# Block-sparse attention followed by a gated MLP: a written-out start for the first two head pairs, small copies moved to Pool, and six output buffers

## The chip, the cores and the metric

The kernel runs on one core of one Trainium2 chip. The metric is the time of one launch in device microseconds (us). Executions of one kernel mostly agree within 0.3%. "Faster" and "slower" mean by more than 2%.

The engines are called PE (TensorE, matmul), DVE (VectorE), ACT (ScalarE), Pool (GpSimd) and SP (SyncE, which here only issues DMAs).

## The reference

```
attention, B=4, H=8, S=768, D=64, chunks of 32 keys:
  k_min, k_max = min, max of k over each chunk
  ub = sum_d max(q*k_min, q*k_max)          # upper bound of a chunk's scores
  ub = -1e9 where the chunk lies after the query's own chunk
  the 6 chunks with the largest ub are kept
  attn = softmax(q k^T / 8 over kept, causal positions);  x = attn v
gated MLP on x (4, 768, 512):
  h = relu(x w_in);  u, v = halves of h
  v = layer-normalised v;  v = w_spatial v + b_spatial   (over the sequence)
  out = (u * v) w_out
```

## The kernel before

The 32 heads are handled as 16 pairs, four to a batch. Each pair has a **preparation** and a **main part**. A table of "beats" (12 to a pair) gives the program order; a scheduler then places the instructions on the engines, and for the first beats it keeps PE's order as written.

Preparation of a pair: PE transposes k; DVE takes the chunk maxima and minima of it (`kmm`); these are copied into a block-diagonal operand (`km`); PE transposes q; its positive and negative parts are taken (`rq`); PE multiplies them to the bounds (`ub`); DVE finds the top six and writes the selection next to q; PE transposes q with its selection, and a copy brings that to SBUF (`a`, two halves). The keys go into `kh`, whose other half holds a constant that turns the selection into a score penalty.

Main part: PE makes scores, ACT takes 12 exps (10 of 128x512 and 2 of 128x128), PE multiplies with v. The causal triangle inside the diagonal blocks is a matmul on PE in batch 0 (pairs 0 to 3), and a selection on Pool from pair 4 on.

```
def init_kh(i):                                   # the constant half of kh
    for hi, (d0, d1) in enumerate(HALF):
        if i < 2:
            nc.scalar.copy(kh_ring[i][hi][d0:d1, :], expand)
        else:
            nc.sync.dma_start(out=kh_ring[i][hi][d0:d1, :], in_=expand)

def k_bounds(self):                               # kmm -> km
    for hi, (d0, d1) in enumerate(HALF):
        copy = nc.gpsimd.tensor_copy if 2 <= self.i < 4 else nc.scalar.copy
        s0, s1 = HALF[1 - hi]
        copy(self.km[d0:d1, :, hi], self.kmm[s0:s1])

def a_copy(self, hi):
    if self.i >= 8: return                        # later pairs: DMA transpose
    copy = nc.vector.tensor_copy if self.i == 0 and hi == 0 else nc.scalar.copy
    copy(self.a[:, :, hi, :], self.tr.rearrange("d (t s) -> d t s", s=P))

def triangle(self, hi):
    if self.b == 0: return                        # batch 0: matmul on PE
    ...
    nc.gpsimd.affine_select(out=blk, in_=blk, ...)

def load_k(g, hi, xy=None):                       # all q, k, v, weight loads: Pool
    ...
    nc.gpsimd.dma_start(out=..., in_=source(k, b, h, 2))

def load_b():
    nc.sync.dma_start(out=b_col, in_=...)         # 768 values of four bytes

def o_group(ti):
    ...
    o_sb = ml.tile([P, DM], F32, tag="o", name="o", bufs=3)
    nc.scalar.copy(o_sb, o_ps)
    nc.sync.dma_start(out=out[b, ti * P:(ti + 1) * P, :], in_=o_sb)
```

The loads convert from 32 to 16 bits. That is why they all stand on Pool: the Trainium skill, "DMA: Bandwidth & Descriptors", section "SWDGE vs HWDGE vs iDMA", says that a DMA that casts can only be issued from GpSimd. The page of this kernel agrees in that its software queue carries all of these loads, 76,512 packets.

The softmax here doesn't subtract the row's maximum and nothing guards it: scores larger than these inputs give would overflow.

Of the kernel before, what the change touches and what calls it, by code (L numbers as in the profile page):

```python
# [10 lines left out]
F32 = mybir.dt.float32  # L11
# [5 lines left out]
P = 128  # L17
# [31 lines left out]
def kernel(  # L49
# [11 lines left out]
    nc = tc.nc  # L61
    B, H, S, D = q.shape
    NCH = S // CHUNK
    DM = H * D
# [14 lines left out]
    ml = ctx.enter_context(tc.tile_pool(name="ml", bufs=2))  # L79
# [14 lines left out]
    beats = defaultdict(list)  # L94

    def at(beat, fn, *args):
        beats[beat].append((fn, args))
# [4 lines left out]
    NB = 4  # L102
# [3 lines left out]
    kh_ring = [[ring.tile([P, S], F16, name=f"kh{i}_{hi}") for hi in range(2)] for i in range(NB)]  # L106
# [40 lines left out]

    def init_kh(i):
        for hi, (d0, d1) in enumerate(HALF):
            if i < 2:  # L150
                nc.scalar.copy(kh_ring[i][hi][d0:d1, :], expand)
            else:
                nc.sync.dma_start(out=kh_ring[i][hi][d0:d1, :], in_=expand)


    W = 2 * NCH
# [3 lines left out]
    class Pair:  # L160
# [26 lines left out]

        def k_bounds(self):
            for hi, (d0, d1) in enumerate(HALF):
                copy = nc.gpsimd.tensor_copy if 2 <= self.i < 4 else nc.scalar.copy  # L190
                s0, s1 = HALF[1 - hi]
                copy(self.km[d0:d1, :, hi], self.kmm[s0:s1])

        def k_operand(self, hi):
            d0, d1 = HALF[1 - hi]
            copy = nc.scalar.copy if self.i == 0 else nc.vector.tensor_copy
            copy(self.kh[hi][d0:d1], self.kT[d0:d1])

        def trans_tile(self):
# [10 lines left out]
        def q_parts(self, m):  # L210
            if m == 0:
                self.rq = sb.tile([P, 2, S], F16, tag="rq", name="rq")
                nc.vector.tensor_scalar(self.rq[:, 0, P:S], in0=self.tr[:, P:S], scalar1=0.0, scalar2=None, op0=Alu.max)
            elif self.i == 0:
                nc.scalar.activation(self.rq[:, 1, P:S], self.tr[:, P:S], func=Act.Relu, scale=-1.0)
            else:
                nc.vector.tensor_scalar(self.rq[:, 1, P:S], in0=self.tr[:, P:S], scalar1=-1.0, scalar2=0.0,
                                        op0=Alu.mult, op1=Alu.max)
# [37 lines left out]
        def a_copy(self, hi):  # L256
            if self.i >= 8:
                return
            copy = nc.vector.tensor_copy if self.i == 0 and hi == 0 else nc.scalar.copy
            copy(self.a[:, :, hi, :], self.tr.rearrange("d (t s) -> d t s", s=P))  # L260


# [109 lines left out]
        nc.vector.tensor_copy(wsT[:, so, :], tr)  # L372

    def load_b():
        nc.sync.dma_start(out=b_col, in_=moe_b_spatial.rearrange("(to ti) -> ti to", ti=P))

    def mlp(b):

        st = {}
        steps = []  # L380

        def matmuls(group, cols, operands, after=None, chunk=2):

            n = len(operands)
            for c0 in range(0, n, chunk):
                def go(c0=c0):
                    if c0 == 0:
                        st[group] = ml_tile()
                    for j in range(c0, min(c0 + chunk, n)):
                        lhsT, rhs = operands[j]()  # L390
                        mm(st[group][:, 0:cols], lhsT=lhsT, rhs=rhs, start=(j == 0), stop=(j == n - 1))  # L391
                    if c0 + chunk >= n:
                        after(st.pop(group))
                steps.append((cols * min(chunk, n - c0), go))

        def v_group(ti):
            def after(h):
                if ti == 0:
                    st["vraw"] = ml.tile([P, NQT, DH], F32, tag="vraw", name="vraw", bufs=1)
                    st["mv"] = ml.tile([P, NQT, nc.vector.BN_AGGR_DIM], F32, tag="mv", name="mv")  # L400
                nc.scalar.activation(st["vraw"][:, ti, :], h, func=Act.Relu)  # L401
                stats = ml.tile([P, nc.vector.BN_STATS_DIM], F32, tag="stats", name="stats")
                nc.vector.bn_stats(stats, st["vraw"][:, ti, :])  # L403
                nc.vector.bn_aggr(st["mv"][:, ti, :], stats)
            matmuls(("v", ti), DH, [lambda ko=ko: (xT[b][:, ko, ti * P:(ti + 1) * P], w_in_sb[:, ko, DH:DFF])
                                    for ko in range(NDO)], after)

        def norm_group(ti):
            def go():
                if ti == 0:  # L410
                    st["rstd"] = ml.tile([P, NQT, 1], F32, tag="rstd", name="rstd")
                    nc.scalar.activation(st["rstd"], st["mv"][:, :, 1:2], func=Act.Ln, bias=eps_t)
                    nc.scalar.activation(st["rstd"], st["rstd"], func=Act.Exp, scale=-0.5)  # L413
                    st["vn"] = ml.tile([P, NQT, DH], F16, tag="vn", name="vn", bufs=1)
                nc.vector.tensor_scalar(st["vn"][:, ti, :], in0=st["vraw"][:, ti, :], scalar1=st["mv"][:, ti, 0:1],  # L415
                                        scalar2=st["rstd"][:, ti, :], op0=Alu.subtract, op1=Alu.mult)
            steps.append((0, go))

        def u_group(ti):
            def after(h):  # L420
                if ti == 0:
                    st["u"] = ml.tile([P, NQT, DH], F16, tag="u", name="u", bufs=1)
                nc.scalar.activation(st["u"][:, ti, :], h, func=Act.Relu)  # L423
            matmuls(("u", ti), DH, [lambda ko=ko: (xT[b][:, ko, ti * P:(ti + 1) * P], w_in_sb[:, ko, 0:DH])
                                    for ko in range(NDO)], after)

        def s_group(ti):
            def after(vs):
                g = ml.tile([P, DH], F16, tag="g", name="g", bufs=3)
                nc.vector.scalar_tensor_tensor(g, in0=vs, scalar=b_col[:, ti:ti + 1], in1=st["u"][:, ti, :],  # L430
                                               op0=Alu.add, op1=Alu.mult)
                gT = st["gT", ti] = ml.tile([P, KO, P], F16, tag="gT", name="gT", bufs=NQT)
                nc.sync.dma_start_transpose(out=gT, in_=g)
            matmuls(("s", ti), DH, [lambda si=si: (wsT[:, si, ti * P:(ti + 1) * P], st["vn"][:, si, :])
                                    for si in range(NQT)], after)

        def o_group(ti):
            def after(o_ps):
                o_sb = ml.tile([P, DM], F32, tag="o", name="o", bufs=3)
                nc.scalar.copy(o_sb, o_ps)  # L440
                nc.sync.dma_start(out=out[b, ti * P:(ti + 1) * P, :], in_=o_sb)
            matmuls(("o", ti), DM, [lambda db=db: (st["gT", ti][:, db, :], w_out_sb[:, db, :])
                                    for db in range(KO)], after)

        def take(fn, *args):
            fn(*args)
            out, steps[:] = list(steps), []
            return out

        v_, u_, n_, s_, o_ = ([take(fn, ti) for ti in range(NQT)]  # L450
                              for fn in (v_group, u_group, norm_group, s_group, o_group))
        return v_, u_, n_, s_, o_


    B0 = -30
# [6 lines left out]
    at(B0, init_ring, 0)  # L462
    at(B0, init_small)
    at(B0, init_expand)
    at(B0, init_masks)
    at(B0, load_k, 0, 0, 1)
    at(B0, load_k, 0, 1, 1)
    at(B0, load_q, 0, 0, 1)
    at(B0, load_q, 0, 1, 1)
    at(B0, load_v, 0)  # L470
    at(B0, init_ring, 1)
    at(-6, init_ring, 2)
    for i in range(NB):
        at(B0 if i < 2 else -8, init_kh, i)
    at(40, load_b)
    for g in range(1, NPAIR // 2):
        t0 = 2 * g * BEATS
# [14 lines left out]
        at(t0 + 18, p.x_transpose)  # L492
    for i, p in enumerate(pairs):
        t0 = i * BEATS
        if i == 1:
            t0 += 4
        if i == 0:
            for step in ((p.k_transpose,), (p.k_max,), (p.k_min,), (p.k_operand, 0), (p.q_transpose,),
                         (p.q_parts, 0), (p.k_bounds,), (p.q_parts, 1), (p.k_operand, 1), (p.bounds,), (p.top, 0), (p.top, 1), (p.select,),
                         (p.a_transpose, 0), (p.a_copy, 0), (p.a_transpose, 1), (p.a_copy, 1)):  # L500
                at(B0 + 1, *step)
            continue
        at(t0 - 27, p.k_transpose)
        at(t0 - 22, p.k_max)
        at(t0 - 21, p.q_transpose)
        at(t0 - 20, p.k_min)
# [10 lines left out]
        at(t0 - 9, p.a_copy, 0)  # L517
        at(t0 - 7, p.a_transpose, 1)
        at(t0 - 6, p.a_copy, 1)
    for j in range(NDO):  # L520
        at(20 + 8 * j, load_w_in, j)
    for j in range(NQT):
# [30 lines left out]
            done += cost  # L553

    with tc.manual_schedule(engines={mybir.EngineType.PE}):
        for beat in sorted(b for b in beats if b < 0):
            for fn, args in beats.pop(beat):
                fn(*args)
    for beat in sorted(beats):
# [31 lines left out]
```

## Time and profile before

Median 211.34 us of three runs before the prediction (211.15 to 211.51); 211.43 with the runs made beside the changed kernel.

The page of the kernel before; busy us, share of the span, number of instructions of each engine:

```profile
PE 187.0 (89%) x1922; PEld 114.8 (55%) x1922; DVE 154.1 (74%) x453; ACT 155.7 (74%) x323; POOL 79.6 (38%) x99
```

An average hides the stages. The table of stretches of the kernel before: each row is a stretch in us, its length, then busy us (and instructions) of PE, PE weight loads, DVE, ACT, Pool, then the clock, DMA share and GB/s.

```profile
0.00:5.00 5.00, 0.00 (x0) 0.00 (x0) 3.34 (x12) 2.11 (x2) 3.79 (x9) 1.00 0.66 37
20.00:25.00 5.00, 3.95 (x59) 3.00 (x59) 4.96 (x21) 3.87 (x9) 2.30 (x4) 1.00 3.52 142
30.00:40.00 10.00, 8.47 (x152) 7.00 (x151) 8.45 (x31) 9.17 (x20) 7.09 (x11) 1.00 2.15 167
40.00:50.00 10.00, 8.84 (x129) 6.45 (x127) 8.86 (x32) 9.36 (x21) 7.66 (x9) 1.00 1.77 176
50.00:58.00 8.00, 7.29 (x103) 5.23 (x102) 6.59 (x15) 7.81 (x18) 7.25 (x9) 1.00 2.01 173
80.00:100.00 20.00, 20.00 (x225) 12.42 (x224) 18.62 (x53) 15.47 (x33) 7.62 (x8) 1.00 1.80 130
120.00:160.00 40.00, 40.00 (x403) 23.54 (x400) 31.41 (x91) 33.61 (x75) 6.63 (x8) 1.00 0.65 119
```

Three regimes: a start in which nothing is full; from about 17 to 58 us attention alone, with ACT and DVE the fullest (38.11 and 36.20 us busy of the 41.30 between 16.7 and 58); then, once the MLP joins in, PE without a gap. From 80 us on only less PE idle time, or less work, can help.

The timeline of the kernel before: start us, duration us, engine, line, operation, output<-input, and in brackets the idle time before and what ended it. First PE's q transposes of pair 0, then ACT from pair 0's last preparation step to pair 1's first exp, then Pool, then the tail.

```profile
9.60 0.69 PE L208 MATMUL trm<-identity,qs_83 128*128 128x128 f16 x5 [2.91 <-DMA qs_83<-in_q_dram]
...
14.99 0.80 ACT L260 COPY a<-trm 128x768 f16<-128x768 f16 x1 [2.76 <-PE trm L254]
16.70 1.57 ACT L274 ACTIVATE e<-sc 128x512 f16<-128x512 f32 x3 [0.90 <-PE sc L272]
18.30 0.48 ACT L192 COPY km_87<-kmm 64x48 f16<-64x48 f16 x2
18.80 2.78 ACT L274 ACTIVATE e<-sc 128x512 f16<-128x512 f32 x6
...
25.46 2.18 ACT L274 ACTIVATE e<-sc 128x512 f16<-128x512 f32 x4
...
50.73 2.04 POOL L330 DMA_DIRECT2D k<-in_k_dram  x2 [0.69 <-PE sc L269]
52.83 0.86 POOL L281 TENSOR_SCALAR_AFFINE_SELECT e<-e 128x768 f16<-128x768 f16 x1
...
202.25 0.59 ACT L440 COPY o<-mlp 128x512 f32<-128x512 f32 x1 [0.28 <-PE mlp L391]
204.32 1.79 ACT L440 COPY o<-mlp 128x512 f32<-128x512 f32 x3 [1.48 <-DMA out_dram<-o]
```

PE waits for q until 9.60; the first exp is at 16.70; the last three output copies wait 1.48 us for one of three buffers to be written out.

### The profile page before, as it was taken

The numbers are of one execution on the slowest core, as the hardware profiler recorded it, in microseconds if no ns is written. First come the engines' busy times: TensorE is split into PE (matmuls) and PEld (weight loads), VectorE is DVE, ScalarE is ACT, GpSimd is POOL, SyncE is SP. The second block draws the span as 40 slices with busy tenths as digits, with TensorE's granted clock in tenths as the row PEclk, the third lists the DMA queues.
The fourth block names the chain that finished last, engine by engine and source line by source line (L and its number), as shares of the span: only waits on it lengthen the run. The fifth ranks groups of instructions, "written<-read, shape, count | busy, mean of one in ns | idle before, by whom it ended". The sixth has DMA issues, their size and how long they took to land.

```text
span 209.2 us, 5074 instructions
## 1 busy us (share of the span) xinstructions
PE 187.0 (89%) x1922; PEld 114.8 (55%) x1922; DVE 154.1 (74%) x453; ACT 155.7 (74%) x323; POOL 79.6 (38%) x99
## 2 busy tenths in 40 slices
PE   0359799798999999999999999999999999999991
PEld 0256577575666665656664656556555554444440
DVE  6348989888889989899888799888547356366520
ACT  4638798999997899785979996668999821666033
POOL 7995697595991364237114111111111110000000
PEclk9999999999999999999999999999999999999998
DMA  6999999999999699979998932948792115530365
GB/s 38 158 128 155 141 172 155 181 177 173 172 163 165 50 117 125 152 128 123 155 258 183 175 55 50 128 86 148 192 172 66 38 28 100 179 147 3 75 157 219
DMA packets 115496, 27.66 MB, mean 132 GB/s; under 512 B 110352, under 2 KB 111888, under 8 KB 115472
## 3 DMA queue, kind: packets, MB, share of 16 engines
q0 software_dynamic: 76512, 12.19, 88.2%
q1 hardware_dynamic: 38960, 15.15, 36.0%
q8 instruction: 15, 0.25, 0.5%
q14 instruction: 9, 0.07, 0.1%
HBM read 24.38 MB, written 6.29 MB: 147 GB/s over the span
## 4 chain that ended last, share of the span: by engine, by line
PE 65%; ACT 17%; DVE 5%; POOL 5%; DMA 4%; issue 3%; POOLq 0%; ACTq 0%
PE mlp L391 38%; PE sc L269 11%; ACT e L274 9%; PE acc L292 8%; ACT a L260 3%; DMA k<-in_k_dram 3%; PE ub L225 2%; POOL qs_83 L341 2%; PE kTp L173 2%; PE tr L208 1%; DVE vn L415 1%; POOL k L332 1%; ACT o L440 1%; DMA out_dram<-o 1%; ACT u L423 1%
## 5 line engine op out<-in xcount | busy, mean ns | idle before, releaser
L274 ACT ACTIVATE e<-sc 128x512 f16<-128x512 f32 x192 | 97.2, 552 | 15.6 <-PE sc L269 13.7
L391 PE MATMUL mlp<-w_in_sb,xT 128*128 128x512 f16 x192 | 52.9, 379 | 0.0
L281 POOL TENSOR_SCALAR_AFFINE_SELECT e<-e 128x768 f16<-128x768 f16 x24 | 20.8, 867 | 68.7 <-ACT e L274 68.6
L292 PEld LDWEIGHTS <-e 128*128 128x128 f16 x672 | 31.6, 97 | 17.5 <-DVE x_2178 L300 1.0
L391 PE MATMUL mlp<-vn,wsT 128*128 128x512 f16 x144 | 37.3, 379 | 0.0
L440 ACT COPY o<-mlp 128x512 f32<-128x512 f32 x24 | 14.1, 590 | 20.8 <-PE mlp L391 18.6
L403 DVE BATCH_NORM_STATS2 stats<-vraw 128x6 f32<-128x512 f32 x24 | 16.6, 693 | 13.5 <-ACT vraw L401 13.1
L391 PE MATMUL mlp<-w_out_sb,gT 128*128 128x512 f16 x96 | 25.1, 379 | 0.0
L391 PEld LDWEIGHTS <-xT 128*128 128x128 f16 x192 | 17.2, 97 | 12.4 <-issue 0.4
L430 DVE SCALAR_TENSOR_TENSOR g<-mlp,b_col,u 128x512 f16<-128x512 f32 x24 | 17.9, 747 | 7.3 <-PE mlp L391 6.2
L391 PEld LDWEIGHTS <-wsT 128*128 128x128 f16 x144 | 12.9, 98 | 10.4
L181 DVE TENSOR_REDUCE kmm<-kTp 128x24 f16<-128x768 f16 x16 | 15.1, 945 | 3.4 <-PE kTp L173 3.2
L401 ACT ACTIVATE vraw<-mlp 128x512 f32<-128x512 f32 x24 | 14.4, 601 | 3.0 <-PE mlp L391 3.0
L423 ACT ACTIVATE u<-mlp 128x512 f16<-128x512 f32 x24 | 14.3, 597 | 1.7 <-PE mlp L391 1.5
L330 POOL DMA_DIRECT2D k<-in_k_dram x14 | 14.4, 1042 | 2.5 <-PE kTp L173 1.8
L185 DVE TENSOR_REDUCE kmm<-kTp 128x24 f16<-128x768 f16 x16 | 15.1, 943 | 0.0
L173 PE MATMUL kTp<-identity,k 128*128 128x128 f16 x96 | 8.6, 230 | 6.3 <-POOL tri L144 5.9
L391 PEld LDWEIGHTS <-gT 128*128 128x128 f16 x96 | 9.1, 98 | 8.9
L292 PE MATMUL acc<-vt_80,e 128*128 128x65 f16 x252 | 13.7, 193 | 0.0
L415 DVE TENSOR_SCALAR vn<-vraw,mv,rstd 128x512 f16<-128x512 f32 x24 | 11.8, 544 | 2.2 <-ACT rstd L413 2.1
L292 PE MATMUL acc<-vt_81,e 128*128 128x65 f16 x252 | 13.0, 193 | 0.2 <-DVE x_3135 L300 0.2
L299 DVE RECIPROCAL rec<-acc 128x6 f32<-128x6 f32 x32 | 6.0, 187 | 6.5 <-PE acc L292 6.2
(165 smaller groups left out, 337.5 us busy)
## 6 DMA issues: line engine op xcount, KB each, us to landing
out_dram<-o SPq DMA_DIRECT2D x24, 256.0 KB, 2.3
k<-in_k_dram POOLq DMA_DIRECT2D x14, 192.0 KB, 8.2
vt_80<-in_v_dram POOLq DMA_DIRECT2D x3, 384.0 KB, 8.7
qs_84<-in_q_dram POOLq DMA_DIRECT2D x6, 192.0 KB, 7.5
vt_81<-in_v_dram POOLq DMA_DIRECT2D x3, 384.0 KB, 8.8
ws_raw<-in_moe_w_spatial_dram POOLq DMA_DIRECT2D x6, 192.0 KB, 7.6
w_in_sb<-in_moe_w_in_dram POOLq DMA_DIRECT2D x8, 128.0 KB, 6.6
qs_85<-in_q_dram POOLq DMA_DIRECT2D x4, 192.0 KB, 7.2
```

The lines of the kernel that those rows point to most:

```text
L181: nc.vector.tensor_reduce(self.kmm[:, 0, :], self.kT.rearrange("d (c ch) -> d c ch", ch=CHUNK), axis=AX.X, op=Alu.max)
L185: nc.vector.tensor_reduce(self.kmm[:, 1, :], self.kT.rearrange("d (c ch) -> d c ch", ch=CHUNK), axis=AX.X, op=Alu.min, negate=True)
L269: mm(sc[:, col:col + n], lhsT=self.kh[hi][:, t * P:(t + 1) * P], rhs=self.a[:, q0 // P:(q0 + n) // P, hi, :], start=True, stop=not diag)
L274: nc.scalar.activation(out=self.e[hi][:, g * 512:g * 512 + width], in_=sc[:, 0:width], func=Act.Exp, scale=scale)
L281: nc.gpsimd.affine_select(out=blk, in_=blk, compare_op=Alu.is_ge, fill=0.0, base=0, channel_multiplier=-1, pattern=[[0, NQT], [1, P]])
L292: mm(self.av[:, qi, :], lhsT=self.e[hi][:, c:c + P], rhs=self.v[hi][:, t, 0:D + 1], start=first and n == 0, stop=last and n == len(blocks) ...
L330: nc.gpsimd.dma_start(out=t[:, :, :, 1 - hi, :].rearrange("p x t d -> p (x t) d"), in_=source(k, b, h, 2))
L391: mm(st[group][:, 0:cols], lhsT=lhsT, rhs=rhs, start=(j == 0), stop=(j == n - 1))
L403: nc.vector.bn_stats(stats, st["vraw"][:, ti, :])
L423: nc.scalar.activation(st["u"][:, ti, :], h, func=Act.Relu)
L430: nc.vector.scalar_tensor_tensor(g, in0=vs, scalar=b_col[:, ti:ti + 1], in1=st["u"][:, ti, :], op0=Alu.add, op1=Alu.mult)
L440: nc.scalar.copy(o_sb, o_ps)
```

## The change

The intent is to shorten the start and to take small work off ACT in the stretch where ACT is full. The core of the diff (the reordering of the beat table is cut):

```
 def init_kh(i):
-            if i < 2:
-                nc.scalar.copy(kh_ring[i][hi][d0:d1, :], expand)
-            else:
-                nc.sync.dma_start(out=kh_ring[i][hi][d0:d1, :], in_=expand)
+            nc.scalar.copy(kh_ring[i][hi][d0:d1, :], expand)
 def k_bounds(self):
-                copy = nc.gpsimd.tensor_copy if 2 <= self.i < 4 else nc.scalar.copy
+                copy = nc.gpsimd.tensor_copy if 1 <= self.i < 8 else nc.scalar.copy
 def a_copy(self, hi):
-            copy = nc.vector.tensor_copy if self.i == 0 and hi == 0 else nc.scalar.copy
+            copy = nc.vector.tensor_copy if self.i < 2 and hi == 0 else nc.scalar.copy
 def load_b():
-        nc.sync.dma_start(out=b_col, ...)
+        nc.gpsimd.dma_start(out=b_col, ...)        # now late, on Pool's queue
 def o_group(ti):
-                o_sb = ml.tile([P, DM], F32, tag="o", name="o", bufs=3)
+                o_sb = ml.tile([P, DM], F32, tag="o", name="o", bufs=6)
 beat table:
-    at(B0, init_masks) before pair 1's k loads;   + after them
-    pair 0 written out, pair 1 by the general table
+    pairs 0 and 1 written out as one list: pair 0's bounds and selection, init_kh(2), init_kh(3),
+    then pair 1's k work between pair 0's two q transposes, pair 1's q work from beat 0 on
-    PE order as written for beats below 0;        + for beats below 6
     [cut: pairs 2 and 3 prepared at other beats]
```

More of the change, by code (lines that the diff above doesn't have):

```diff
@@ L195, in k_operand @@
             d0, d1 = HALF[1 - hi]
-            copy = nc.scalar.copy if self.i == 0 else nc.vector.tensor_copy
+            copy = nc.scalar.copy if self.i < 1 else nc.vector.tensor_copy
             copy(self.kh[hi][d0:d1], self.kT[d0:d1])
@@ L213, in q_parts @@
                 nc.vector.tensor_scalar(self.rq[:, 0, P:S], in0=self.tr[:, P:S], scalar1=0.0, scalar2=None, op0=Alu.max)
-            elif self.i == 0:
+            elif self.i < 1:
                 nc.scalar.activation(self.rq[:, 1, P:S], self.tr[:, P:S], func=Act.Relu, scale=-1.0)
@@ L374, in load_b @@
     def load_b():
-        nc.sync.dma_start(out=b_col, in_=moe_b_spatial.rearrange("(to ti) -> ti to", ti=P))
+        nc.gpsimd.dma_start(out=b_col, in_=moe_b_spatial.rearrange("(to ti) -> ti to", ti=P))
     def mlp(b):
@@ L464 @@
     at(B0, init_expand)
-    at(B0, init_masks)
     at(B0, load_k, 0, 0, 1)
     at(B0, load_k, 0, 1, 1)
+    at(B0, init_masks)
     at(B0, load_q, 0, 0, 1)
@@ L471 @@
     at(B0, init_ring, 1)
-    at(-6, init_ring, 2)
-    for i in range(NB):
-        at(B0 if i < 2 else -8, init_kh, i)
+    at(B0, init_ring, 2)
+    at(B0, init_kh, 0)
+    at(B0, init_kh, 1)
     at(40, load_b)
@@ L494 @@
         t0 = i * BEATS
-        if i == 1:
-            t0 += 4
-        if i == 0:
-            for step in ((p.k_transpose,), (p.k_max,), (p.k_min,), (p.k_operand, 0), (p.q_transpose,),
-                         (p.q_parts, 0), (p.k_bounds,), (p.q_parts, 1), (p.k_operand, 1), (p.bounds,), (p.top, 0), (p.top, 1), (p.select,),
-                         (p.a_transpose, 0), (p.a_copy, 0), (p.a_transpose, 1), (p.a_copy, 1)):
-                at(B0 + 1, *step)
+        if i < 2:
             continue
-        at(t0 - 27, p.k_transpose)
+        t0 += 4 if i < 4 else 0
+        at(t0 - (22 if i < 4 else 27), p.k_transpose)
         at(t0 - 22, p.k_max)
@@ L519 @@
         at(t0 - 6, p.a_copy, 1)
+    p, n = pairs[0:2]
+    for beat, *step in (
+            (B0 + 1, p.k_transpose), (B0 + 1, p.k_max), (B0 + 1, p.k_min), (B0 + 1, p.k_operand, 0),
+            (B0 + 1, p.q_transpose), (B0 + 1, p.q_parts, 0), (B0 + 1, p.k_bounds),
+            (B0 + 1, p.q_parts, 1), (B0 + 1, p.k_operand, 1), (B0 + 1, p.bounds), (B0 + 1, p.top, 0),
+            (B0 + 1, p.top, 1), (B0 + 1, p.select), (B0 + 1, init_kh, 2), (B0 + 1, init_kh, 3), (B0 + 1, p.a_transpose, 0), (B0 + 1, p.a_copy, 0),
+            (B0 + 1, n.k_transpose), (B0 + 1, p.a_transpose, 1), (B0 + 1, n.k_max), (B0 + 1, p.a_copy, 1), (B0 + 1, n.k_min),
+            (B0 + 1, n.k_operand, 0),
+            (0, n.q_transpose), (1, n.q_parts, 0), (1, n.k_bounds), (1, n.q_parts, 1),
+            (1, n.k_operand, 1), (2, n.bounds), (3, n.top, 0), (3, n.top, 1), (4, n.select), (5, n.a_transpose, 0),
+            (5, n.a_copy, 0), (6, n.a_transpose, 1), (6, n.a_copy, 1)):
+        at(beat, *step)
     for j in range(NDO):
@@ L555 @@
     with tc.manual_schedule(engines={mybir.EngineType.PE}):
-        for beat in sorted(b for b in beats if b < 0):
+        for beat in sorted(b for b in beats if b < 6):
             for fn, args in beats.pop(beat):
```

## The prediction

> **What bounds the kernel now.** Busy table: PE 187.0 of 209.2 us; the 22 us of idle PE lie mostly at the front. Table of stretches and timeline show three regimes. (a) 0 to 16.7 us, start-up: the first exp starts at 16.70; PE waits 2.9 us for pair 0's q, until 9.6. (b) 16.7 to 58 us, attention alone: ACT about 94% busy, DVE nearly as full (4.96 and 4.97 of 5 us in 20:25 and 25:30; the chain of waits is DVE from 19.7 to 24). (c) 58 to 201 us: PE-bound (20.00 of 20, 40.00 of 40). At the end ACT waits 1.48 us for an output DMA (three buffers).
>
> Time taken out of (a) and (b) should carry to the end; nothing taken off ACT in (c) should.
>
> **The change, costed from the trace.**
> 1. Four SP copies of the key constants (96 KB each, issued 4.2 to 6.6 us) become four ACT copies of 0.83 us. They stand after pair 0's key operand (ends 12.2), where ACT idles 2.76 us before 14.99: nearly free. The bias load leaves the start too. The Trainium skill, "Trainium Kernel Development and Optimization", Key Constraints, says that DMAs of all queues share 16 engines and interleave; the trace fits: a q load of pair 0 beside those copies took 4.9 us, later ones 3.6 to 3.8. q may land up to 1 us earlier; I count 0.4.
> 2. PE order: the first scores come straight after pair 0's transposes instead of after pair 1's q transposes: gain 0.3. Against it, pair 1's bounds matmuls stand before the fourth score tile; ACT should wait about 1.3 us near 18 to 19.4.
> 3. Pair 1's first a-copy goes from ACT (0.80) to DVE (0.56), and pairs 1, 4, 5, 6, 7 send their bounds copies (2 x 0.24 us) to Pool. ACT loses 3.2 us in (b). As DVE is as full, I expect about half to count: pair 1's first exp from 25.46 to about 24.2, start of the MLP from 58.4 to about 56.
> 4. Pool waits in order for the key reductions, so some loads issue 1 to 2 us later; later pairs' loads have many us of slack.
> 5. Six output buffers take away the 1.48 us wait; PE then sets the last copies, which end about 205.45 instead of 206.11: gain 0.65.
>
> Sum: 0.7 (start) + 0.6 (pair 0 to pair 1) + 1.3 (rest of b) + 0.65 (tail) = 3.3 us.
>
> **Predicted time: 208.0 us, 8 in 10 between 205.8 and 210.3. Faster by over 2% (below 207.1) 0.29, within 2% 0.68, slower by over 2% 0.03.**
>
> **What would show it.** (1) The wait of the first q transposes ends before 9.3; first exp at 15.6 to 16.5. (2) An ACT gap of about 1.3 us after pair 0's third exp; pair 1's first exp near 24.2. (3) First ReLU of the MLP at about 56; ACT's bounds copies 18 instead of 28; DVE at least 95% busy between 15 and 40. (4) No PE wait over 1 us for a k, q or v load after 20 us. (5) No output copy waiting for an output DMA at the end; PE busy still about 187.
>
> **What would make it wrong.** Pool's in-order waits hold up a load that is needed. ACT's gap in pair 0 is larger, because pair 1's select or pair 2's k comes late. DVE alone sets the pace in (b), and the ACT savings buy nothing. Or q lands a full microsecond earlier and DVE keeps up: then about 206.

## The result, and the profile after

The changed kernel takes 209.04 us (median of four, 208.90 to 209.11) against 211.43 before. The ratio is 0.9884, with a 95% interval of 0.9865 to 0.9903. (A ratio here is the mean time of one kernel's fast runs over that of the other's of the same rounds, so not quite the ratio of the medians.) A later control, the same kernel on the chip of the last experiments, gave 0.9887. So it gained 2.4 us, inside the predicted range, less than the 3.3 us of the predicted sum.

The page of the changed kernel:

```profile
PE 189.0 (91%) x1922; PEld 115.4 (56%) x1922; DVE 154.5 (75%) x454; ACT 155.7 (75%) x316; POOL 82.6 (40%) x110
```

PE's busy time rose by 2.0 us with the same 1922 matmuls, while the kernel got faster. The Trainium skill, "Trainium Kernel Development and Optimization", section "Performance Expectations", warns that matmul busy time is a bad metric for how close a kernel is to roofline, because matmuls are pipelined. The busy time did not follow the work. PE busy is used below to see where PE is full, not as an amount of work.

The table of stretches of the changed kernel:

```profile
20.00:25.00 5.00, 4.61 (x69) 3.45 (x68) 4.82 (x13) 4.75 (x11) 3.84 (x8) 1.00 3.67 141
30.00:40.00 10.00, 9.08 (x137) 6.66 (x135) 9.89 (x36) 8.52 (x18) 8.03 (x14) 1.00 2.13 168
50.00:58.00 8.00, 6.94 (x101) 4.92 (x100) 6.36 (x21) 6.50 (x13) 6.61 (x10) 1.00 2.02 173
80.00:100.00 20.00, 20.00 (x220) 12.48 (x218) 18.73 (x53) 15.34 (x33) 6.86 (x7) 1.00 1.58 132
```

Two rows matter. In 30:40 DVE is now full (9.89 of 10) and ACT is not. In 50:58 ACT fell from 7.81 to 6.50, and no engine is full: something makes them wait.

The timeline of the changed kernel (its source lines are three lower than before's):

```profile
8.02 0.69 PE L205 MATMUL trm<-identity,qs 128*128 128x128 f16 x5 [1.48 <-DMA qs<-in_q_dram]
...
14.59 0.80 ACT L257 COPY a<-trm 128x768 f16<-128x768 f16 x1
15.29 0.60 ACT L271 ACTIVATE e<-sc 128x512 f16<-128x512 f32 x1
18.55 3.21 ACT L271 ACTIVATE e<-sc 128x512 f16<-128x512 f32 x7 [1.23 <-PE sc L266]
22.02 0.80 ACT L257 COPY a<-trm 128x768 f16<-128x768 f16 x1 [0.25 <-PE trm L251]
22.71 5.44 ACT L271 ACTIVATE e<-sc 128x512 f16<-128x512 f32 x12
...
50.85 2.04 POOL L327 DMA_DIRECT2D k<-in_k_dram  x2 [0.80 <-DMA k<-in_k_dram]
52.95 0.86 POOL L278 TENSOR_SCALAR_AFFINE_SELECT e<-e 128x768 f16<-128x768 f16 x1
53.86 0.36 PE L289 MATMUL acc<-vt,e 128*128 128x65 f16 x6 [0.55 <-POOL e L278]
54.48 1.09 ACT L271 ACTIVATE e<-sc 128x512 f16<-128x512 f32 x2 [1.34 <-PE sc L266]
...
202.60 0.58 ACT L437 COPY o<-mlp 128x512 f32<-128x512 f32 x1 [0.28 <-DMA out_dram<-o]
203.46 0.58 ACT L437 COPY o<-mlp 128x512 f32<-128x512 f32 x1 [0.28 <-PE mlp L388]
```

q is there at 8.02, the first exp starts at 15.29. (The 12 exps from 22.71 are the last two of pair 0 and the first ten of pair 1.) In the tail the copies are paced by PE: the 0.28 us gaps are those of the earlier copies, so the label of the first one does not name what set its start.

The lines at 50 to 55 us are the new thing. Read them from the bottom. ACT waits 1.34 us for pair 5's scores. Those stand behind six value matmuls of pair 4 in PE's queue, which wait for Pool's selection of the causal triangle. The selection stands in Pool's queue behind two key loads of 2.04 us in all. Those keys are for pairs 10 and 11; PE first reads them at 85.61 us. The chain of waits of the changed kernel (from the last instruction back, at each step to what released it) says the same. It adds that Pool stood idle for 0.80 us before those loads; this profile puts the wait down to the landing of an earlier key load (the control, 0.62 us, to PE's scores):

```profile
41.57 1.42 POOL vt L343
42.99 7.32 DMA k<-in_k_dram
...
50.85 0.44 POOL k L327
51.87 1.02 POOL k L327
52.95 0.87 POOL e L278
53.86 0.36 PE acc L289 x6
54.22 0.23 PE sc L266
54.48 1.09 ACT e L271 x2
```

To follow the gain through the kernel, take the start of each pair's first exp, found by counting twelve exps to a pair in ACT's timeline (us, profiled runs):

| | before | changed | gain |
|---|---|---|---|
| pair 0 | 16.70 | 15.29 | 1.41 |
| pair 1 | 25.46 | 23.36 | 2.10 |
| pair 4 | 49.16 | 46.75 | 2.41 |
| pair 5 | 55.94 | 54.48 | 1.46 |
| pair 6 | 68.04 | 66.52 | 1.52 |
| pair 8 | 89.03 | 88.18 | 0.85 |
| pair 10 | 109.01 | 107.63 | 1.38 |
| pair 15 | 160.03 | 158.65 | 1.38 |
| end of last output copy | 206.11 | 204.05 | 2.06 |

The start won more than predicted, and by pair 4 the kernel was 2.4 us ahead. Between pairs 4 and 5 it lost 0.95 us of that. Another 0.67 us went between pairs 6 and 8, and 0.53 came back between pairs 8 and 10; both are taken up below. The tail added 0.7. (This execution of the kernel before took 210.93 us, a little less than its median.)

### The profile page after: what moved, and what is told of

The parts are those of the page before. It is cut to its first block, busy times and chain, and to the rows that moved or that the text cites. A ratio compares the mean times of both kernels' runs of the same rounds, so it can differ in the third digit from the quotient of the medians.

```text
span 207.3 us, 5072 instructions
## 1 busy us (share of the span) xinstructions
PE 189.0 (91%) x1922; PEld 115.4 (56%) x1922; DVE 154.5 (75%) x454; ACT 155.7 (75%) x316; POOL 82.6 (40%) x110
## 4 chain that ended last, share of the span: by engine, by line
PE 69%; ACT 12%; DVE 8%; DMA 5%; issue 2%; POOL 2%; ACTq 0%; POOLq 0%; DVEq 0%
PE mlp L388 41%; PE sc L266 11%; PE acc L289 7%; ACT e L271 7%; DMA k<-in_k_dram 5%; PE kTp L170 2%; DVE kmm L178 2%; PE ub L222 2%; PE trm L251 1%; ACT a L257 1%; DVE vn L412 1%; ACT u L420 1%; DVE kmm L182 1%; PE tr L205 1%; DVE max L232 1%
## 5 line engine op out<-in xcount | busy, mean ns | idle before, releaser
L266 PE MATMUL sc<-a,kh 128*128 128x512 f16 (+3 forms) x256 | 65.8, 308 | 1.4 <-ACT e L271 0.8
L289 PE MATMUL acc<-vt,e 128*128 128x65 f16 x672 | 35.3, 194 | 0.9 <-POOL e L278 0.6
L266 PEld LDWEIGHTS <-kh 128*128 128x128 f16 x256 | 22.6, 98 | 13.7 <-issue 1.0
L232 DVE MAX8 max<-ub 128x8 f32<-128x8 f32 (+4 forms) x160 | 15.4, 164 | 5.0 <-PE ub L222 4.9
L178 DVE TENSOR_REDUCE kmm<-kTp 128x24 f16<-128x768 f16 x16 | 15.1, 944 | 3.7 <-PE kTp L170 2.7
L297 DVE TENSOR_TENSOR x<-acc,rec 128x384 f16<-128x384 f32 x32 | 17.6, 551 | 0.3
L336 POOL DMA_DIRECT2D qs<-in_q_dram x14 | 14.4, 1037 | 6.8 <-PE sc L266 3.2
L194 DVE COPY kh<-kTp 64x768 f16<-64x768 f16 x30 | 16.5, 549 | 0.5
```

Of the source, the lines that this page charges most:

```text
L178: nc.vector.tensor_reduce(self.kmm[:, 0, :], self.kT.rearrange("d (c ch) -> d c ch", ch=CHUNK), axis=AX.X, op=Alu.max)
L194: copy(self.kh[hi][d0:d1], self.kT[d0:d1])
L232: nc.vector.max(self.max8[:, qi - 1, hi, :], ub[:, c0:c0 + CPT * (qi + 1)])
L266: mm(sc[:, col:col + n], lhsT=self.kh[hi][:, t * P:(t + 1) * P], rhs=self.a[:, q0 // P:(q0 + n) // P, hi, :], start=True, stop=not diag)
L289: mm(self.av[:, qi, :], lhsT=self.e[hi][:, c:c + P], rhs=self.v[hi][:, t, 0:D + 1], start=first and n == 0, stop=last and n == len(blocks) ...
L297: nc.vector.tensor_tensor(self.x16[:, :, hi, :], in0=self.av[:, :, 0:D], in1=rec.to_broadcast([P, NQT, D]), op=Alu.mult)
```

## The experiments

The theory after reading the trace, called P below: Pool's in-order queue of loads sets when pair 4's first triangle selection starts, and with it pair 5. What is won before is cut off there. The rival, A, is the prediction's own: half of ACT's saved time counts. Twelve kernels ran, all correct. Each is compared with before, on the same chip.

### The bounds copies back on ACT

```
-  copy = nc.gpsimd.tensor_copy if 1 <= self.i < 8 else nc.scalar.copy
+  copy = nc.gpsimd.tensor_copy if 2 <= self.i < 4 else nc.scalar.copy     # rest as changed
```

> The changed kernel with the block-diagonal bounds copies of pairs 1, 4, 5, 6 and 7 back on ACT (10 copies of 0.23 us); everything else as changed. Theory A, as in the prediction (half of the ACT time taken off between 17 and 58 us counts): slower than the changed kernel by about 1.2 us, so about 1.2 us faster than before (ratio 0.994). Theory B, from the changed kernel's trace (after 28 us its chain of waits is DVE, and ACT idles about 3.5 us between 28 and 40; at 53 us the chain goes through Pool's queue of loads to the first triangle selection, so ACT time is free there): the same as the changed kernel within 0.4 us (ratio 0.987 to 0.990), and the first ReLU of the MLP at 56 to 57 us. Theory C: the copies on Pool hold up the loads, so taking them off makes it faster than the changed kernel by over 0.4 us and the first triangle selection of pair 4 starts clearly before 52.9.

Measured: 208.80 us, ratio 0.9880 (0.9859 to 0.9901); the first ReLU of the MLP at 57.28, a little later than B said. At the end, undoing this part costs nothing, which is not what A says. C falls too. Pair 4 starts at 47.31 instead of 46.75, so the copies did help by 0.6 us there. But the selection starts at 52.95 in both, and pair 5 at 54.85 instead of 54.48 (54.74 in the control further down). The lead of 0.1 to 0.4 us that the changed kernel still has there is lost between pairs 6 and 8, where this kernel is faster by 0.68 us. That second place is described after the experiments.

### The bounds copies on Pool, alone

```
-  copy = nc.gpsimd.tensor_copy if 2 <= self.i < 4 else nc.scalar.copy     # rest as before
+  copy = nc.gpsimd.tensor_copy if 1 <= self.i < 8 else nc.scalar.copy
```

> The kernel before with one edit: the bounds copies of pairs 1 to 7 on Pool. If ACT is what bounds the stretch from 17 to 58 us (prediction: half counts), 0.8 to 1.2 us faster than before (ratio 0.994 to 0.996). If DVE and Pool's loads set the pace: within 0.4 us of before (0.998 to 1.002).

Measured: 209.67 us, ratio 0.9926 (0.9902 to 0.9950), 1.6 us faster. This is more than either expectation. That is two thirds of the 2.3 us taken off ACT (ten copies of 229 ns). The profiles show less: 0.97 us at pair 5 and 1.18 us at the last output copy. So by the measured times the same edit gives 1.6 us alone and nothing beside the new start.

The Trainium skill, "GPSIMD Engine Reference", section "Engine selection", says one-input work runs at roughly line rate on Pool, while Pool has no access to PSUM. No run here put these copies on DVE; beside ACT, Pool is no slower at this size: a 64x48 copy takes 218 ns on Pool and 229 on ACT. It can move because `kmm` lies in SBUF.

### Three output buffers again

```
-  o_sb = ml.tile([P, DM], F32, tag="o", name="o", bufs=6)                 # rest as changed
+  o_sb = ml.tile([P, DM], F32, tag="o", name="o", bufs=3)
```

> The changed kernel with three output buffers instead of six. If the tail gain is the wait for an output buffer alone: slower than the changed kernel by 0.6 to 0.7 us (ratio to before about 0.9915), ACT waits about 1.5 us for an output DMA near 202 us, and everything before about 200 us stands as in the changed kernel. If the buffers mattered earlier too, the start of the last MLP stretch would move as well.

Measured: 210.20 us, ratio 0.9940 (0.9916 to 0.9964), 1.2 us slower than the changed kernel by the difference of the ratios. The order of instructions is identical on every engine, so the buffers are worth about 1.2 us, not the 0.65 of the tail. Two later pairs of kernels with identical orders say the same: 1.2 us (0.9926 against 0.9870) and 1.0 us (0.9926 against 0.9880).

The rest is found near 110 us. There the kernel before has an output copy that waits 0.5 us for a buffer; PE, otherwise full, leaves the chain of waits for five microseconds. Pieces of that chain in the kernel before (start, length, what):

```profile
108.84 0.77 ACT e L274 x2
109.61 0.50 ACT vraw L401
110.13 0.69 DVE stats L403
...
112.18 0.40 DVE rq L213
113.11 0.57 DVE x_2178 L300
113.72 0.45 PE acc L292 x9
```

The delayed ACT work delays a string of DVE work, and PE waits for its end. From pair 9's to pair 10's first exp it takes 9.87 or 9.88 us in the changed kernel and the runs with the bounds copies on ACT, the early bias and the operands on ACT (all with six buffers). With three buffers it takes 10.41 us before, 10.22 with the bounds copies alone, 10.18 here and 9.94 with the new start alone; in these four ACT sits idle before the fourth output copy for 0.48, 0.29, 0.25 and 0.01 us. So a short wait of an engine that is not the bottleneck came out at about its own length, 0.1 to 0.5 us, and how large it is depends on when the copy arrives.

### The constants by DMA again

```
-            nc.scalar.copy(kh_ring[i][hi][d0:d1, :], expand)              # rest as changed
+            if i < 2: nc.scalar.copy(kh_ring[i][hi][d0:d1, :], expand)
+            else:     nc.sync.dma_start(out=kh_ring[i][hi][d0:d1, :], in_=expand)
```

> The changed kernel with the key constants of pairs 2 and 3 copied by SP DMAs again, instead of by ACT; the bias stays late. Theory A (those four DMAs delay pair 0's q): the wait of the first q transposes ends at about 9.4 us instead of 8.0, the first exp starts about 0.9 us later than 15.3, and pair 1's first exp later as well; at the end 0.3 to 0.9 us is lost against the changed kernel. Rival: q's landing came earlier because the bias load (768 packets of four bytes) left the start, and the constants have nothing to do with it: then q still lands at about 8.0 and the time is that of the changed kernel within 0.3 us.

Measured: 209.50 us, ratio 0.9909 (0.9889 to 0.9929). The timeline of this kernel:

```profile
10.11 0.69 PE L208 MATMUL trm<-identity,qs 128*128 128x128 f16 x5 [3.58 <-DMA qs<-in_q_dram]
```

The first q transposes start 2.1 us later than in the changed kernel (1.5 us later than in the latest of the ten profiles with the constants on ACT, which give 7.90 to 8.57), and the first exp starts at 16.84, 1.55 us later. So the four constant DMAs delay q. The second q load is issued at 4.54 in both kernels and lands at 9.97 here, at 7.89 in the changed kernel. This fits the Trainium skill's statement, quoted in the prediction, that DMAs of all queues share 16 engines and interleave. Yet at the end only 0.5 us is lost. Pair 4 starts 1.2 us later than in the changed kernel, pair 5 only 0.5 us: the loss is forgiven where the gain was cut off.

### The bias early again

```
-        nc.gpsimd.dma_start(out=b_col, ...)                               # rest as changed
+        nc.sync.dma_start(out=b_col, ...)
```

> The changed kernel with the bias load on SP at the start again. Its 768 packets of four bytes run before the first key load lands. If the bias had a share in q's landing at 8.0 instead of 9.6, the first q transposes start 0.2 us or more later than 8.4 (the run with the constants by ACT and the bias late gave 8.0 to 8.6 in four profiles). If the constants alone did it, q's landing stays in 8.0 to 8.6. Either way the end time stays within 0.4 us of the changed kernel, because pair 5 is pinned by Pool.

Measured: 208.57 us, ratio 0.9858 (0.9832 to 0.9885). q is there at 7.90, at the early end of the other profiles with this start (8.02 to 8.57), so the bias had no share in q's delay. The issue of the late bias load occupied Pool for 0.85 us at 36 us; with it gone, Pool's selection comes at 52.45 instead of 52.95 (53.21 in the control), and pair 5 at 53.98 instead of 54.48 (54.74). That is what P says, from the other side. The time is about 0.6 us better than the changed kernel's, more than the 0.4 expected; the intervals overlap, so it is not shown that this version is faster.

### Pair 4's triangle on PE

```
-  diag = self.b == 0 and si == 0          +  diag = self.i < 5 and si == 0
-  if self.b == 0: return                  +  if self.i < 5: return         # in triangle()
```

> The changed kernel, with pair 4's causal triangle put into its scores by PE (12 more 128-wide matmuls of about 0.055 us issue time, 0.7 us) as for pairs 0 to 3, instead of by two selections on Pool. The first selection on Pool is then pair 5's. Theory P (Pool's queue of loads pins pair 5: in five kernels the first selection starts at 52.8 to 53.4 and pair 5's first exp at 54.5 to 55.9, although pair 4's first exp ranges from 46.5 to 49.2): pair 5's first exp comes 1 us or more before 54.5, ACT's wait of 1.34 us there is gone, and the whole is 0.3 to 1.3 us faster than the changed kernel after paying PE's 0.7 us. Rival (pair 5 is late because its own select on DVE or the PE order makes it so, and Pool only happens to end then): pair 5's first exp stays at 54 to 55 and the time is equal or up to 0.7 us slower.

Measured: 208.67 us, ratio 0.9856 (0.9829 to 0.9883). The timeline of this kernel:

```profile
53.99 0.60 ACT L271 ACTIVATE e<-sc 128x512 f16<-128x512 f32 x1 [0.50 <-PE sc L266]
```

ACT's wait falls from 1.34 to 0.50 us. Pair 4 to pair 5 takes 6.6 us instead of 7.7. Pair 5 comes only 0.5 us earlier, not the full microsecond expected; pair 4 itself began 0.6 us later here. Neither forecast holds in full: the wait shrinks, as P says, but pair 5 comes just where the rival's range begins (53.98 us was also reached by the early bias, with the selections on Pool). So Pool set the last wait, and something else of pair 5 stands close behind it. After paying for PE's 12 extra matmuls the kernel is about 0.6 us ahead of the changed one, again within overlapping intervals.

### Three key operands on ACT

```
-  copy = nc.scalar.copy if self.i < 1 else nc.vector.tensor_copy
+  copy = nc.scalar.copy if self.i < 1 or (2 <= self.i < 5 and hi == 1) else nc.vector.tensor_copy
```

> The changed kernel with three DVE copies (the second key operand of pairs 2, 3 and 4, 0.56 us each) moved to ACT (0.79 us each), which idles about 3.5 us between 28 and 40. If DVE sets the pace between 20 and 40 us, pair 3's first exp comes before 39.5 (39.76 and 40.00 in two kernels with the same start) and pair 4's before 46.5. If ACT does, they come later by up to 2 us. Because of Pool's pin the end time moves by at most 0.5 us in both cases.

Measured: 208.58 us, ratio 0.9857 (0.9830 to 0.9883). Pair 3 starts at 39.44, which the DVE theory asked for, but the changed kernel's own order gave 39.46 to 39.76 in five profiles, so this shows nothing. Pair 4 starts at 47.41, later than the 46.5 it asked for. So DVE is not alone in setting the pace between 20 and 47 us. Neither expectation holds in full, and the end time moved by about 0.6 us, more than expected; in the profile this kernel gains 0.68 us between pairs 6 and 8 (see below).

### Two key buffers

```
-  name="k", bufs=3)                       +  name="k", bufs=2)             # rest as changed
```

> The changed kernel with two buffers instead of three for the key tiles. In the instruction order this moves the key loads of pairs 10 and 11 (50.9 to 52.9 us in the changed kernel) behind pair 4's selections, but brings three more output-weight loads ahead of the first selection. Theory P: what stands ahead of the first selection in Pool's queue sets it; 2.0 us of key loads go and 1.65 us of weight loads come, so it starts at 51.5 to 53 and the whole moves by at most 0.5 us. If it starts over 1 us earlier, pair 5's first exp must come earlier by as much.

Measured: 214.82 us, ratio 1.0148 (1.0104 to 1.0191), slower by 1.5%. The first selection did not come at 51.5 to 53 but at 53.84, since each of the weight loads that moved ahead of it had waits of its own. Pair 5 followed to 55.37, as P requires. But the 6 us lost against the changed kernel were not lost there. The waits of this kernel between 40 and 120 us (who waited for whom: us in total, times, longest):

```profile
POOL vt L343 <- PE sc L266: 9.8, 3, 8.3
PE sc L266 <- DMA a<-qs: 3.9, 1, 3.9
```

PE waits 3.9 us for a DMA transpose of `a`, in the stretch from 101 to 112 us, on which the chain of waits puts 11.33 us. Key loads that the smaller pool had put off stand at 97.3 to 99.3 us in Pool's timeline, just before it; they land at 107.43 and 112.11. That the loads and the transpose compete for the DMA engines would fit this; no run tested it.

### The control, and the parts combined

The changed kernel unaltered, as control:

> The changed kernel itself, unaltered, as a control on the same chip and beside the same runs of before as the three others. Ratio to before 0.986 to 0.991.

Measured: 208.89 us, ratio 0.9887 (0.9870 to 0.9904).

Bounds copies on Pool and six buffers, with the old start:

```
-  2 <= self.i < 4  ...  bufs=3            +  1 <= self.i < 8  ...  bufs=6   # rest as before
```

> The kernel before with two of the edits, the bounds copies of pairs 1 to 7 on Pool and six output buffers, and its own start-up. Theory P (the start's gain is swallowed before pair 5, and the buffers are worth 0.3 to 0.5 us near 105 us and 0.65 us in the tail): about 2.7 us faster than before, ratio 0.986 to 0.989, as fast as the changed kernel, although its first exp comes 1.5 us later. If the written-out start is what carries the change: ratio 0.992 or more.

Measured: 208.50 us, ratio 0.9870 (0.9849 to 0.9891). Two one-line edits give the whole gain, although this kernel's first exp starts at 16.47 and pair 4's at 47.77, 1.2 us after those of the control.

The new start alone:

```
-  1 <= self.i < 8  ...  bufs=6            +  2 <= self.i < 4  ...  bufs=3   # rest as changed
```

> The changed kernel with both other edits undone: bounds copies as before, three output buffers. Only the written-out start with the constants by ACT, the late bias and pair 1's a-copy on DVE is left. Theory P, not additive: 1.2 to 1.6 us faster than before (0.9925 to 0.9945), from which together with the bounds alone (0.9926) and the buffers (1.1 us) the sum would be over 4 us, whereas the changed kernel gains 2.4. If the parts are additive, this run must be within 0.4 us of before, because bounds (1.6) and buffers (1.1) already make up the whole.

Measured: 209.68 us, ratio 0.9926 (0.9907 to 0.9946), 1.6 us faster than before. So the parts are worth, alone: start 1.6, bounds 1.6, buffers 1.0 to 1.2 us; sum 4.2 to 4.4. Together: 2.4. Start and buffers without bounds: 2.5 (0.9880). Bounds and buffers without start: 2.7. The buffers add to either. Start and bounds do not add to each other: together, without the extra buffers (the run with three output buffers), they give 1.3 us (0.9940).

The two edits that looked best, together:

> The changed kernel with pair 4's triangle on PE and the second key operands of pairs 2 to 4 on ACT, the two edits that gave 0.9856 and 0.9857 alone. If each takes away its own idle PE time, it is 0.5 to 1.2 us faster than the changed kernel beside it (ratio 0.982 to 0.986). If both uncover the same next limit, it is equal to either alone within 0.3 us.

(edit: the triangle of pair 4 on PE and the three operands on ACT, as above)

Measured: 209.31 us, ratio 0.9901 (0.9885 to 0.9916), worse than either alone. The timeline of this kernel:

```profile
54.23 0.80 ACT L257 COPY a<-tr 128x768 f16<-128x768 f16 x1 [1.00 <-PE tr L251]
```

With Pool out of the way, pair 5 starts at 55.57. It now waits for its own preparation: in the chain of waits DVE's q parts and x copy, then PE's transposes, then this ACT copy. So the next limit stands within about a microsecond of Pool's (54.48 and 54.74 in the changed kernel and its control), and PE's added matmuls are paid on top. No version was found that is clearly faster than the changed kernel.

### The selection and pair 5, in all of them

All numbers in us, from the profiles. "Ready" is the end of the sixth exp of pair 4, after which the first selection could start. "Late" is how long after that it starts. The last column is the time from the end of the selection to pair 5's first exp. The two runs with pair 4's triangle on PE have no such selection.

| kernel | pair 4 | ready | selection | late | pair 5 | selection to pair 5 |
|---|---|---|---|---|---|---|
| before | 49.16 | 52.14 | 52.83 | 0.69 | 55.94 | 2.25 |
| bounds alone | 48.60 | 51.57 | 53.30 | 1.73 | 54.97 | 0.81 |
| constants by DMA | 47.95 | 50.89 | 53.40 | 2.51 | 54.95 | 0.70 |
| bounds and buffers | 47.77 | 50.74 | 52.99 | 2.24 | 54.57 | 0.73 |
| operands on ACT | 47.41 | 50.38 | 52.74 | 2.36 | 54.32 | 0.73 |
| bounds on ACT | 47.31 | 50.34 | 52.95 | 2.61 | 54.85 | 1.04 |
| start alone | 47.16 | 50.19 | 53.39 | 3.21 | 54.92 | 0.67 |
| changed | 46.75 | 49.69 | 52.95 | 3.26 | 54.48 | 0.67 |
| changed, control | 46.60 | 49.54 | 53.21 | 3.67 | 54.74 | 0.67 |
| bias early | 46.52 | 49.45 | 52.45 | 3.00 | 53.98 | 0.67 |
| three buffers | 46.45 | 49.65 | 53.25 | 3.60 | 54.78 | 0.67 |
| two key buffers | 46.63 | 49.57 | 53.84 | 4.27 | 55.37 | 0.67 |

Pair 4 spans 2.7 us; the selection stays within 1 us and does not follow it, except with two key buffers, where the edit changed Pool's queue itself. (The changed kernel, its control and the run with three buffers have identical instruction orders, so their 52.95, 53.21 and 53.25 show how far profiles differ.) Where the selection is late by 3.0 us or more, pair 5 follows its end by 0.67 us, always. This is a floor for pair 5: a kernel that arrives later pays less for it, and a kernel that arrives earlier gains nothing there.

The floor is not the whole reason why start and bounds do not add. Against before, the start alone is 1.14 us ahead at pair 6, the bounds alone 0.99, both with six buffers 1.52: about 0.6 us is missing. At pair 8 the three numbers are 1.14, 0.99 and 0.85: 1.3 us is missing. So about half goes at a second place, which no experiment was made for but the profiles show. From pair 6's to pair 8's first exp takes 21.66 or 21.67 us in the changed kernel and in the five runs in which PE executes its matmuls in the same order as there (control, bias early, three buffers, constants by DMA, two key buffers). It takes 20.98 to 21.00 us in the eight others. PE executes the same 240 matmuls in this stretch in either order and shows no more idle time (0.45 us in the changed kernel, 0.50 with the bounds on ACT), so the loss is hidden in its busy time. The scheduler chose the order; taking the bounds copies back to ACT, or moving the operands or the triangle, gave it another one. That the order costs the 0.67 us is read from which kernels share it; no run changed the order alone, and why it costs time is open.

A queue like the one at pair 4 also stands at pair 8. With pair 4's triangle on PE, pair 8's first selection is ready at 91.12, but starts at 94.31, behind two q loads of 2.04 us in all, and PE waits 0.70 us for it. From pair 8's to pair 9's first exp takes 10.44 us there, against 9.57 or 9.58 in all kernels with pair 4's triangle on Pool.

## Why the prediction was right or wrong

The total was right: 208.0 predicted, 209.04 measured, in the range and within 2%. The terms of its sum were not all right. In the profiles they are 1.4 us (start), 0.7 (pair 0 to pair 1), -0.3 (from there to the MLP's first ReLU), -0.4 (from there to pair 15) and 0.7 (tail), 2.1 in all, where the prediction had 0.7, 0.6, 1.3, 0 and 0.65. The larger start made up for part of what was lost later, so that the total came this close was in part luck.

1. **Start, predicted gain 0.7 us.** Right in its mechanism, too small. q came 1.6 us earlier, and the first exp 1.41 us earlier. The cause was the one named, the constants' DMAs (shown by putting them back). The bias had no part in it.
2. **"ACT should wait about 1.3 us near 18 to 19.4".** Right: 1.23 us, ended at 18.55, behind pair 1's bounds matmuls as predicted. Pair 1's first exp was predicted near 24.2 and came at 23.36.
3. **"ACT loses 3.2 us ... I expect about half to count", a further 1.3 us between pair 1 and the MLP.** This is the step that failed. Up to pair 4 the gain grew by only 0.3 us; between pairs 4 and 5 it lost 0.95. From pair 1 to the MLP's first ReLU the gain fell from 2.10 to 1.80 us, where the prediction added 1.3. The prediction took ACT's and DVE's fullness as the limit of the whole stretch. The runs showed a third limit at its end: Pool's queue, late by 3.3 us with pair 4's selection. In the kernel before, it was late by 0.69 us and the six value matmuls behind it did not hold up pair 5, so the profile of before could not show it as a wait of any size. A second part of the loss, 0.67 us between pairs 6 and 8, goes with the order of PE's matmuls and lies in the PE-bound stretch, where the prediction let every gain "carry to the end". The first had to be looked for: what becomes the next constraint if everything before it moves up by 2 us?
4. **"Later pairs' loads have many us of slack".** True of the loads, and still the wrong question. No load was late for PE. The risk named in the prediction, that Pool's waits "hold up a load that is needed", had the right queue and the wrong victim: not a load but a computing instruction that shares the queue.
5. **Buffers, predicted 0.65 us.** The tail did as said (the last copies end 4.90 us after the nineteenth one starts, before 5.59). But the whole is 1.0 to 1.2 us in three comparisons. "Nothing taken off ACT in (c) should" carry was too strong: near 110 us a wait of ACT for a buffer, 0.48 us in the kernel before, came through DVE to PE at about its full length.
6. **The signs.** ACT's bounds copies fell from 28 to 18, and the first ReLU came at 56.61, as said. The first exp, at 15.29, came before the range of 15.6 to 16.5, and PE busy was 189.0 instead of about 187. DVE was not "at least 95% busy between 15 and 40": the rows of the full table (3.68, 4.82, 3.70 and 9.89 us) sum to 22.1 of 25 us, 88%.

What stays open: whether it is PE's order that costs 0.67 us between pairs 6 and 8, and why it would, and whether the three edits that gave 0.9856 to 0.9858 are really faster than the changed kernel with its 0.9884, since the intervals overlap. The profiles say where each would have it from: the early bias at pair 5 (0.5 us), the operands on ACT between pairs 6 and 8 (0.68), the triangle on PE at both places (0.5 and 0.67), of which 0.87 is lost again between pairs 8 and 9.

## What to carry to other kernels

When two edits shorten the same stretch, look for what is clocked by something else at its end; here it was a queue of loads that hardly followed the gain, and each edit alone, or both, brought pair 5 to nearly the same place. Then follow the gain to the end of the kernel: a second loss here came along with another order of the same matmuls. An in-order queue that both issues loads and computes needs the same scrutiny as a bottleneck engine even when it is 40% busy, because a load needed 35 us later can stand in front of a computation needed now. And test the parts of a bundled change alone: about half of this gain was one number, the count of output buffers.

## What the Trainium skill lacked or had wrong

- "GPSIMD Engine Reference", section "Common operations": it lists issuing DMAs and memory operations such as `tensor_copy` for the engine, but not, in that section or among its pitfalls, that a load's issue holds up computation behind it. Here issuing one 192 KB load took 1.03 us of Pool's timeline, and two of them stood before a selection of 0.86 us that was ready 3.3 us earlier.
- "DMA: Bandwidth & Descriptors", section "Rules for kernel authors": its advice to issue DMAs early has a price that is not named beside it. Two loads issued at 50.85 and first read at 85.61 stood before pair 4's selection, and four constant copies beside the first loads delayed q by 1.5 to 2.1 us.
- "Perfetto Trace Analysis", section "Identifying the Most-Contended Engine": the section has the engine with the highest occupancy taken as the one to improve, with PE judged otherwise. Between 50 and 58 us this is weak guidance: in the changed kernel it gives Pool, but with 6.61 of 8 us against 6.50 for ACT and 6.36 for DVE, and in the kernel before it gives ACT, 7.81 against Pool's 7.25. The chain of waits showed Pool plainly.
